# Four weight tiles parted into two words ahead of their use

## The chip, the cores and the metric

The kernel runs on one core of one Trainium2 chip. The core has five engines with queues of their own: TensorE (PE, with its weight loads PEld), VectorE (DVE), ScalarE (ACT), GpSimd (POOL) and SyncE (SP, which here only issues transfers). The metric is the device time of one launch in microseconds (us).

## What is computed

Three layers stand behind each other, on 8 batches of 576 positions and 512 features:

```
q_p, k_p = phi(q), phi(k)                 # exp(+-(x @ w_phi - max|.|)), 256 features per head
attn  = (q_p @ (k_p^T v)) / (q_p @ sum k_p + 1e-6)
gate  = sigmoid(causal depthwise convolution of attn, 5 taps)
x     = (gate * (attn @ w_val)) @ w_out
u     = x + real(fft over positions and features of x)
un    = (u - mean) / sqrt(var + 1e-6)      # over the 512 features
out   = u + relu(un @ w_ch1) @ w_ch2       # 512 -> 2048 -> 512
```

The weights `w_val`, `w_out`, `w_ch1` and `w_ch2` arrive as 64-bit floats and are made into 32-bit ones on the chip. Every product of the second and third layer works on operands parted into two words: a high word `h` in the rounded type fp32r, and a low word `l = x - h`. One product is then three matmuls, h*h, h*l and l*h (`mm3`, L77).

## The kernel before

**Stages.** The attention (`run_attention`, L1162) runs in 80 steps of a written order, and beside it all weights are converted and stored to DRAM (`conv_mlp`, L324, into `w_scr`). Then comes the mixing, a loop over batches (L1242 to L1265): for batch b+1 the convolution taps, the sigmoid and the value product (`emit_V`), for batch b the output product (`emit_W`) and the two transforms (`emit_FD`, `emit_SD`). The mixing's order on each engine is found by the tile framework, which may move an instruction past others of its engine. The last turn of that loop is `run_last` (L1001), called the tail below: transforms and output product of the last two batches, the layer norm of the first block of 512 positions (`ln_stages`) and its operands (`prep_un`). After it `run_mlp` (L1152) walks 9 blocks of 512 positions twice, once for each half of the 2048 hidden features.

**Weights of the MLP.** Each of the two MLP products multiplies 2x2 blocks with seven products in place of eight, so that a weight tile of four 128x128 quarters needs four sums of quarters beside them: `sum_w` (L329) loads the four quarters of a tile (columns 0 to 511 of a row of `w_scr`), forms the sums on POOL in place (L339 to L342), and stores all four results behind the quarters (L343). There are 32 tiles (product i, column group j of 8, half o), five after each batch of the mixing, with a buffer `ws` of two slots. Columns 128 to 1023 are the seven operands, 896 columns.

**Parting.** `prep_w` (L660) loads such a row into a buffer `wr` (two slots, a counter alternates them), rounds it to the high word on ACT (`o_hi`, L640, recorded at L66) and subtracts on DVE or POOL (`o_lo`, recorded at L72 for DVE, at L75 for POOL). In `run_last` it is called for column groups 0 and 1 of the first product, which the first MLP products need (two calls, four tiles, L1013 and L1014), and for group 2 (L1020). The rest is parted in the first block and at the change of halves.

**Order in the tail and the MLP.** `run_last` and `run_mlp` write down operations with the engines that may do them ("v" DVE, "p" POOL, "a" ACT, "d" SP's queue, "m" PE), and `place_ops` (L1071) puts them into an order by due times: of the operations that are ready on an engine, the one that is due first goes first. An operation marked "vp" is given to POOL when POOL, at twice the duration, would end it before DVE could get to it, or before it is due. The first MLP products write PSUM tiles that take the place of the tail's (`open_mlp2`), and the tail's last DVE operations read those.

**Buffers around the change.** The pool `g` holds the taps' sum `acc` (its own slots, used in the attention only; later a PSUM tile `psa` with one slot takes its place, L415), the sigmoid `sg` (two slots), its product with the values `gv` (two) and the sums and differences `gs` (two). `ident` is the identity matrix for the attention's transposes.

Of the kernel before, what the change touches and what calls it, by code (L numbers as in the profile page):

```python
# [7 lines left out]
F32 = mybir.dt.float32  # L8
F32R = mybir.dt.float32r
# [3 lines left out]
ALU = mybir.AluOpType  # L13
# [4 lines left out]
NB, NH, S, D, F = 8, 8, 576, 64, 128  # L18
DM, DFF, KC = 512, 2048, 5
NT = NB * S  # L20
HS = S // 2
# [8 lines left out]
def f32(ap):  # L30
    return ap.bitcast(F32)
# [3 lines left out]
def attention_moe_mixer_kernel(  # L35
# [18 lines left out]
    nc = tc.nc  # L54
    mm = nc.tensor.matmul

    def pool(stack, name, bufs, space=None, side=None):
        kw = {} if space is None else {"space": space}
        if side is not None:
            kw["side"] = side  # L60
        if space is not DRAM:
            kw["reuse_waits"] = "tile"
        return stack.enter_context(tc.tile_pool(name=name, bufs=bufs, **kw))

    def hi_act(dst, src):
        nc.scalar.activation(out=dst, in_=src, func=ACTF.Copy)  # L66
# [7 lines left out]
    def lo_pool(dst, src, hi):  # L74
        nc.gpsimd.tensor_tensor(out=dst, in0=src, in1=f32(hi), op=ALU.subtract)  # L75
# [8 lines left out]
    def convert(i, src, n, shape, halve, done):  # L84
        raw = P["xf"].tile([128, 1024, 2], I32, tag="xf", name="raw64")[:, 0:n]
        nc.sync.dma_start(out=raw.rearrange("p n t -> p (n t)").rearrange("p (k f) -> p k f", k=shape[0]), in_=src)
        yield
        lo32, hi32 = raw[:, :, 0].bitcast(U32), raw[:, :, 1]
        a = P["xh"].tile([128, 2, 1024], I32, tag=f"x{i % 2}", name="cv")
        ex, lo = a[:, 0, 0:n], f32(a[:, 1, 0:n])  # L90
        sg = lo
        mt = stg.tile([128, 1024], I32, tag="mt", name="mt")[:, 0:n]
        w = f32(mt)
        nc.vector.tensor_scalar(out=ex, in0=hi32, scalar1=0x7FF00000, scalar2=None, op0=ALU.bitwise_and)
        nc.scalar.activation(out=lo, in_=lo32, func=ACTF.Copy, scale=2.0 ** -32)
        yield
        nc.vector.tensor_scalar(out=mt, in0=hi32, scalar1=0xFFFFF, scalar2=0x4B000000, op0=ALU.bitwise_and, op1=ALU.bitwise_or)  # L97
        nc.scalar.activation(out=ex, in_=ex, func=ACTF.Relu, scale=8.0, bias=ebias[:, int(halve):int(halve) + 1])
        nc.gpsimd.tensor_scalar(out=w, in0=w, scalar1=-7340032.0, scalar2=None, op0=ALU.add)  # L99
        nc.gpsimd.tensor_tensor(out=w, in0=lo, in1=w, op=ALU.add)  # L100
        yield
        nc.scalar.activation(out=sg, in_=hi32, func=ACTF.Sign)
        nc.gpsimd.tensor_tensor(out=w, in0=w, in1=f32(ex), op=ALU.mult)
        nc.gpsimd.tensor_tensor(out=w, in0=w, in1=sg, op=ALU.mult)
        done(w.rearrange("p (k f) -> p k f", k=shape[0]))
        yield

    base = pool(ctx, "base", 1)
    ebias = base.tile([128, 2], F32, name="ebias")
    dram = pool(ctx, "scratch", 1, DRAM)  # L110
    ident = base.tile([128, 128], F32, name="ident")
    eps = base.tile([128, 1], F32, name="eps")
    warm = base.tile([128, 1], F32, name="warm")
    ones = base.tile([128, 128], F32R, name="ones")
    x_scr = [dram.tile([4, 128, S], F32, name=f"x_scr{b}") for b in range(NB)]
    w_scr = [dram.tile([NJ, 2, 128, 8 * 128], F32, name=f"w_scr{i}") for i in range(2)]
    un_scr = [dram.tile([128, 4, TB], F32, name=f"un_scr{t}") for t in range(NBK)]
    part_scr = [[dram.tile([128, 2, HB], F32, name=f"part_scr{t}_{q}") for q in range(4)] for t in range(NBK)]
    u_scr = [dram.tile([4, 128, S], F32, name=f"u_scr{b}") for b in range(NB)]
# [4 lines left out]
    P = {"g1": pool(ctx, "g1", 1)}  # L124
# [19 lines left out]
    vx = ExitStack()  # L144
    gx = ExitStack()
    lx = ExitStack()
    R = "right"
# [10 lines left out]
    ap1 = pool(att, "ap1", 1)  # L158
# [6 lines left out]
    ps_nm = pool(att, "ps_nm", 1, PSUM)  # L165

    wp = ap1.tile([128, F], F32, name="wp")

    raw = {}
    pj = {}  # L170
# [153 lines left out]
    def conv_mlp(n, j, i):  # L324
        def done(t):
            nc.sync.dma_start(out=w_scr[i][j][:, :, 0:512].rearrange("o p f -> p o f"), in_=t)
        return convert(n, (w_ch1, w_ch2)[i][j].bitcast(I32).rearrange("o p f -> p o f"), 1024, (2,), False, done)

    def sum_w(n):  # L329
        for k in ((0, 1) if n == 0 else (n + 1,)):  # L330
            if k < len(wsteps):
                i, j, o = wsteps[k]
                wsum[k] = t = P["ws"].tile([128, 512], F32, tag="ws", name="ws")
                nc.sync.dma_start(out=t, in_=w_scr[i][j, o][:, 0:512])
        i, j, o = wsteps[n]
        t = wsum.pop(n)
        a21, a11, a12, a22 = (t[:, k * 128:(k + 1) * 128] for k in range(4))
        tt = nc.gpsimd.tensor_tensor
        tc.keep_in_program_order(tt(out=a22, in0=a21, in1=a22, op=ALU.add))  # L339
        tt(out=a21, in0=a11, in1=a21, op=ALU.subtract)  # L340
        tt(out=a11, in0=a22, in1=a11, op=ALU.subtract)
        tt(out=a12, in0=a12, in1=a11, op=ALU.subtract)  # L342
        nc.sync.dma_start(out=w_scr[i][j, o][:, 512:1024], in_=t)  # L343

    def conv_taps(i):
        def done(t):
# [23 lines left out]
    def open_mix():  # L370
        P["g0"] = pool(gx, "g0", 1, side=R)
        P["ws"] = pool(vx, "ws", 2, side=R)
        P["psv"] = pool(vx, "psv", 2, PSUM, side=R)
        P["psa"] = pool(vx, "psa", 1, PSUM, side=R)

# [11 lines left out]

    wsteps = [(i, j, o) for j in range(NJ) for i in range(2) for o in range(2)]
    wsum = {}
    xf = {}  # L390
    xhl = {}
    geo = {}
# [20 lines left out]
    def tap_steps(b, m):  # L413
        x = xf[b]
        if "psa" in P:  # L415
            acc = P["psa"].tile([128, 2, 512], F32, tag="pa", name="acc")[:, :, 0:HS]
        else:
            acc = P["g"].tile([128, 2, HS], F32, tag="acc", name="acc")

        def shifted(t):  # L420
            return x[:, m, t:t + S].rearrange("p (a s) -> p a s", a=2)
        nc.scalar.activation(out=acc, in_=shifted(4), func=ACTF.Copy, scale=cw[:, m, 4:5])  # L422
        for t in range(4):
            nc.vector.scalar_tensor_tensor(  # L424
                out=acc, in0=shifted(t), scalar=cw[:, m, t:t + 1], in1=acc, op0=ALU.mult, op1=ALU.add
            )
            if t < 3:
                yield
        taps[b, m] = acc
        yield  # L430

    def emit_taps(b, m):
        drain(tap_steps(b, m))

    def emit_V(b, m):
        h, l = xhl[b]
        if m == 0:
            geo[b] = tuple(P[f"g{b % 2}"].tile([128, 4, 2, NE], F32R, tag=f"g{i}", name="ge") for i in range(2))
        if (b, m) not in taps:
            emit_taps(b, m)  # L440
        t = taps.pop((b, m))
        acc = P["g"].tile([128, S], F32, tag="sg", name="sg")
        nc.scalar.activation(out=acc.rearrange("p (a s) -> p a s", a=2), in_=t, func=ACTF.Sigmoid)
        gv = P["g"].tile([128, S + 2], F32, tag="gv", name="gv")
        for n in range(2):
            p = P["psv"].tile([128, HS], F32, tag="ps", name="val")
            sl = slice(n * HS, (n + 1) * HS)
            for c in range(4):
                ws = slice(m * 128, (m + 1) * 128)
                mm3(p, (wv[0][:, c, ws], wv[1][:, c, ws]), (h[:, c, sl], l[:, c, sl]), c == 0, c == 3)  # L450
            nc.vector.tensor_tensor(out=gv[:, sl], in0=p, in1=acc[:, sl], op=ALU.mult)
        nc.vector.tensor_copy(out=gv[:, S:S + 1], in_=gv[:, 0:1])
        gs = P["g"].tile([128, 2, NE], F32, tag="gs", name="gs")
        for a, op in ((0, ALU.add), (1, ALU.subtract)):
            nc.vector.tensor_tensor(out=gs[:, a, :], in0=gv[:, 0:NE], in1=gv[:, S:S - NE:-1], op=op)  # L455
        gh, gl = geo[b]
        hi_act(gh[:, m], gs)
        lo_pool(gl[:, m], gs, gh[:, m])
        if m == 3:
            xhl.pop(b)  # L460
            xf.pop(b)
# [115 lines left out]
    NJP = NJ // 2  # L577
    NH_SLOTS = 7
    blocks = [(0, t) for t in range(NBK)] + [(1, t) for t in reversed(range(NBK))]
    wt = [[], []]  # L580
# [71 lines left out]
    def o_dma(pairs, r, w, kb, e="d"):  # L652
        def f(e):
            for o, x in pairs:
                (nc.sync if e == "d" else nc.scalar).dma_start(out=o, in_=x)
        op(e, 0, f, r, w, max(0.5 * len(pairs), K["bw"] * kb) if e == "d" else 0.5 * len(pairs), K["dl"] + 0.0028 * kb)
# [2 lines left out]

    def prep_w(i, j, e):  # L660
        for o in range(2):
            b = wcount[0] % 2
            wcount[0] += 1
            h, l = wt[i][j % NJP][o]
            raw = wr[b]
            r = raw.rearrange("p q f -> p (q f)")
            wk = [("w", i, j % NJP, o, k) for k in range(2)]
            o_dma([(r, w_scr[i][j, o, :, 128:1024])], [], [("wr", b)], 448)
            o_hi(h, raw, 896, [("wr", b)], [wk[0]])
            o_lo(e, l, raw, h, 896, [("wr", b), wk[0]], [wk[1]])  # L670
            yield
# [699 lines left out]
```

## Time and profile before

| | |
|---|---|
| runs timed | 1438.33, 1440.83, 1443.11 us, median 1440.83 |
| the profiled execution | 1442.91 us |
| its span, first to last instruction | 1441.1 us |
| granted TensorE clock, mean | 0.979 of full speed |
| PE / PEld busy | 1352.5 us (94%) / 1301.8 us (90%) |
| DVE busy | 1247.2 us (87%) |
| ACT busy | 814.1 us (56%) |
| POOL busy | 707.0 us (49%) |
| transfers | 187 MB, 130 GB/s in the mean |

How to read it: the busy shares are means over stages that have different limits. The attention ends near 340 us, the mixing runs to about 607 us, the tail from there to about 657 us, and the MLP from there to the end. All times in rows are microseconds from the start of the span, unless they are marked ns.

### The profile page before, as it was taken

The page shows a single profiled execution, that of the slowest core. Times are in us where ns is not written, and L with a number is a line of the kernel's source. Part 1 is how long each engine was busy: PE and PEld are TensorE (multiplying, and loading weights), DVE is VectorE, ACT ScalarE, POOL GpSimd, SP SyncE. Part 2 cuts the span into 40 slices and gives each one's busy share as a digit, 9 for nine tenths or more (in the row PEclk, how much of TensorE's full clock was granted, in tenths as well). Part 3 has the DMA queues.
Part 4 walks back from the last instruction along what each step waited for, and adds up shares of the span by engine and source line. Part 5 has one row for each costly group of instructions (what it writes and reads, how often), then busy time and mean ns, then how long its engine had stood idle before and what let it go on. Part 6 is the DMA issues. An engine that isn't in the chain of part 4 may idle for free.

```text
span 1441.1 us, 35040 instructions
## 1 busy us (share of the span) xinstructions
PE 1352.5 (94%) x14672; PEld 1301.8 (90%) x14672; DVE 1247.2 (87%) x1938; ACT 814.1 (56%) x1513; POOL 707.0 (49%) x526
## 2 busy tenths in 40 slices
PE   6899999997999999986899899999999999999998
PEld 5788888887999999986899899999999999999998
DVE  6689999886999989798999999999899887788776
ACT  4778888764545545464555555555555555444442
POOL 3858888721667666563655655545436111111111
PEclk9999999998999999988899999999999999999999
DMA  6457777741333432236322332232343222222211
GB/s 231 148 187 252 270 273 267 244 173 35 132 133 140 144 135 100 91 112 214 132 89 89 118 104 87 75 116 89 116 125 101 81 81 66 83 88 89 88 38 51
DMA packets 89851, 186.98 MB, mean 130 GB/s; under 512 B 10455, under 2 KB 37335, under 8 KB 87518
## 3 DMA queue, kind: packets, MB, share of 16 engines
q1 hardware_dynamic: 88488, 181.33, 37.0%
q10 hardware_dynamic: 1206, 3.41, 0.6%
q8 instruction: 115, 1.88, 0.5%
q14 instruction: 42, 0.34, 0.1%
HBM read 121.79 MB, written 62.93 MB: 128 GB/s over the span
## 4 chain that ended last, share of the span: by engine, by line
PE 44%; DVE 32%; issue 7%; POOL 7%; ACT 5%; DMA 4%; SPq 0%; DVEq 0%; POOLq 0%; ACTq 0%
PE cx L875 9%; PE x L806 9%; PE cy L875 5%; PE y L806 4%; DVE acc L424 4%; DVE A L647 3%; DVE c L647 3%; PE kv L243 3%; PE z L806 3%; PE nm L282 2%; DVE acc L647 2%; PE pj L204 2%; PE cz L875 2%; DVE s L751 2%; DVE gs L455 2%
## 5 line engine op out<-in xcount | busy, mean ns | idle before, releaser
L875 PE MATMUL cx<-h,w 128*128 128x256 f32 x1152 | 176.2, 286 | 4.8 <-ACT h L66 2.5
L875 PEld LDWEIGHTS cx<-h,w 128*128 128x128 f32 x1152 | 158.2, 194 | 6.7 <-ACT h L66 3.1
L66 ACT ACTIVATE h<-c 128x512 fp32r<-128x512 f32 x180 | 111.6, 627 | 39.7 <-DVE c L647 22.4
L647 POOL TENSOR_TENSOR c<-c,c 128x512 f32<-128x512 f32 x35 | 49.8, 1422 | 165.2 <-ACT h L650 125.6
L647 DVE TENSOR_TENSOR acc<-cx,acc 128x512 f32<-128x512 f32 x144 | 98.0, 681 | 33.7 <-PE cx L875 33.0
L650 ACT ACTIVATE c<-c 128x512 f32<-128x512 f32 x108 | 67.9, 630 | 99.9 <-DVE c L647 98.5
L806 PE MATMUL x<-un,w 128*128 128x256 f32 x864 | 117.2, 285 | 6.5 <-DVE eo L647 5.8
L75 POOL TENSOR_TENSOR h<-c,h 128x512 fp32r<-128x512 f32 x33 | 48.3, 1466 | 149.2 <-ACT h L66 149.0
L875 PE MATMUL cy<-h,w 128*128 128x256 f32 x864 | 117.3, 284 | 3.1 <-DVE h L72 1.9
L806 PEld LDWEIGHTS x<-un,w 128*128 128x128 f32 x864 | 109.9, 193 | 7.2 <-issue 6.0
L424 DVE SCALAR_TENSOR_TENSOR acc<-xf,cw,acc 128x576 f32<-128x576 f32 x128 | 105.0, 820 | 11.9 <-ACT acc L422 10.8
L875 PEld LDWEIGHTS cy<-h,w 128*128 128x128 f32 x864 | 108.9, 191 | 5.6 <-DVE h L72 2.5
L243 PE MATMUL kv<-vraw,ke 128*64 128x66 f32 x2560 | 97.2, 229 | 13.8 <-ACT ke L222 11.1
L243 PEld LDWEIGHTS kv<-vraw,ke 128*64 128x64 f32 x2560 | 84.4, 140 | 25.7 <-ACT ke L222 12.0
L72 DVE TENSOR_TENSOR h<-c,h 128x512 fp32r<-128x512 f32 x111 | 103.9, 937 | 1.3 <-ACT h L66 0.7
L211 DVE TENSOR_REDUCE m<-pj 128x8 f32<-128x1024 f32 (+1 forms) x80 | 88.7, 1108 | 10.3 <-PE pj L204 10.3
L204 PE MATMUL pj<-wp,kqraw 64*128 64x128 f32 x1152 | 88.8, 292 | 5.4 <-DMA kqraw<-in_k_dram 4.4
L204 PEld LDWEIGHTS pj<-wp,kqraw 64*128 64x128 f32 x1152 | 73.0, 192 | 19.2 <-issue 18.1
L214 DVE TENSOR_TENSOR y<-pj,m 128x1024 f32<-128x1024 f32 (+1 forms) x80 | 88.7, 1108 | 0.4
L282 PE MATMUL nm<-kvT,qe 128*64 128x65 f32 x2304 | 84.6, 226 | 3.1 <-DVE xs L293 1.6
L75 POOL TENSOR_TENSOR ge<-gs,ge 128x580 fp32r<-128x580 f32 x32 | 46.8, 1462 | 78.7 <-ACT ge L66 78.7
L99 POOL TENSOR_SCALAR mt<-mt 128x1024 f32<-128x1024 f32 (+1 forms) x21 | 55.7, 2651 | 59.9 <-DVE mt L97 42.5
(249 smaller groups left out, 4244.0 us busy)
## 6 DMA issues: line engine op xcount, KB each, us to landing
raw<-in_w_ch_dram SPq DMA_DIRECT2D x16, 1024.0 KB, 7.1
wr<-w_scr SPq DMA_DIRECT2D x32, 448.0 KB, 3.5
vraw<-in_v_dram SPq DMA_DIRECT2D x16, 660.0 KB, 8.6
x_scr<-xT SPq DMA_DIRECT2D x32, 288.0 KB, 5.9
xf<-x_scr SPq DMA_DIRECT2D x8, 1152.0 KB, 5.9
out_dram<-acc SPq DMA_DIRECT2D x36, 256.0 KB, 2.2
kqraw<-in_k_dram SPq DMA_DIRECT2D x15, 576.0 KB, 7.7
kqraw<-in_q_dram SPq DMA_DIRECT2D x15, 576.0 KB, 6.2
```

Of the source, the lines that this page charges most:

```text
L66: nc.scalar.activation(out=dst, in_=src, func=ACTF.Copy)
L72: nc.vector.tensor_tensor(out=dst, in0=src, in1=f32(hi), op=ALU.subtract)
L75: nc.gpsimd.tensor_tensor(out=dst, in0=src, in1=f32(hi), op=ALU.subtract)
L204: mm(p[:, h, o:o + F], t[r, w, 128 * c:128 * c + 128], wp[r, :], start=True, stop=True)
L211: nc.vector.tensor_reduce(out=m, in_=pv, axis=AX.X, op=ALU.max, apply_absolute_value=True)
L214: nc.vector.tensor_tensor(out=y, in0=pv, in1=m.unsqueeze(3).to_broadcast([128, 2, 2 * n, F]), op=ALU.subtract)
L243: mm(t[p, w, :], e[:, a, h, j, p], tv[:, h, slot, :], start=slot % 5 == 0 and w == 0, stop=slot % 5 == 4 and w == 3, skip_group_check=True)
L282: mm(t[p, 2 * j + h, 0:65], e[:, a, h, j, p], kt[:, 2 * h + a, b, :], start=(a == 0), stop=(a == 1))
L424: nc.vector.scalar_tensor_tensor(out=acc, in0=shifted(t), scalar=cw[:, m, t:t + 1], in1=acc, op0=ALU.mult, op1=ALU.add)
L647: op(e, cols, lambda e: (nc.vector if e == "v" else nc.gpsimd).tensor_tensor(out=o, in0=x, in1=y, op=alu), r, w)
L806: mm(p[:, n], l, v[:, kt], start=first and n + kt + m == 0, stop=kt == 1 and m == 2, skip_group_check=True)
L875: mm(p[:, o], v, r[:, n], start=first and o + n + m == 0, stop=n + m == 3, skip_group_check=True)
```

## The change

The four tiles of the first product's column groups 0 and 1 (the test is `parted`, L331 of the changed kernel) are parted during the mixing. `sum_w` puts its four sums behind the quarters in a buffer `ws` that is twice as wide (1024 columns, still two slots) and stores only the sums. For the four tiles it stores nothing; it rounds columns 128 to 1023 into a new buffer `wh` (one slot) on ACT. The next call of `sum_w` begins with `part_w`: POOL subtracts in place, and SP stores both words to a new DRAM scratch `w_hl`. Only then the next tile's load is issued. `prep_w` has for these tiles two plain loads of the words straight into their places, without ACT, DVE, POOL or `wr`.

To make room, three tiles give way: `ident` lies in a pool that ends with the attention, the taps' `acc` of the attention takes slots of `gv`, and the sigmoid `sg` has one slot in place of two.

```diff
--- before.py
+++ after.py
@@ -108,12 +108,12 @@
     base = pool(ctx, "base", 1)
     ebias = base.tile([128, 2], F32, name="ebias")
     dram = pool(ctx, "scratch", 1, DRAM)
-    ident = base.tile([128, 128], F32, name="ident")
     eps = base.tile([128, 1], F32, name="eps")
     warm = base.tile([128, 1], F32, name="warm")
     ones = base.tile([128, 128], F32R, name="ones")
     x_scr = [dram.tile([4, 128, S], F32, name=f"x_scr{b}") for b in range(NB)]
     w_scr = [dram.tile([NJ, 2, 128, 8 * 128], F32, name=f"w_scr{i}") for i in range(2)]
+    w_hl = [dram.tile([2, 2, 2, 128, 7 * 128], F32, name="w_hl0")]
     un_scr = [dram.tile([128, 4, TB], F32, name=f"un_scr{t}") for t in range(NBK)]
     part_scr = [[dram.tile([128, 2, HB], F32, name=f"part_scr{t}_{q}") for q in range(4)] for t in range(NBK)]
     u_scr = [dram.tile([4, 128, S], F32, name=f"u_scr{b}") for b in range(NB)]
@@ -165,6 +165,7 @@
     ps_nm = pool(att, "ps_nm", 1, PSUM)
 
     wp = ap1.tile([128, F], F32, name="wp")
+    ident = ap1.tile([128, 128], F32, name="ident")
 
     raw = {}
     pj = {}
@@ -326,21 +327,44 @@
             nc.sync.dma_start(out=w_scr[i][j][:, :, 0:512].rearrange("o p f -> p o f"), in_=t)
         return convert(n, (w_ch1, w_ch2)[i][j].bitcast(I32).rearrange("o p f -> p o f"), 1024, (2,), False, done)
 
+
+    def parted(i, j):
+        return i == 0 and j < 2
+
+    def load_ws(n):
+        if n < len(wsteps):
+            i, j, o = wsteps[n]
+            wsum[n] = t = P["ws"].tile([128, 1024], F32, tag="ws", name="ws")
+            nc.sync.dma_start(out=t[:, 0:512], in_=w_scr[i][j, o][:, 0:512])
+
+    def part_w():
+        if parting:
+            i, j, o, r, h = parting.pop()
+            l = r.bitcast(F32R)
+            lo_pool(l, r, h)
+            nc.sync.dma_start(out=w_hl[i][j, o, 0], in_=f32(h))
+            nc.sync.dma_start(out=w_hl[i][j, o, 1], in_=f32(l))
+
     def sum_w(n):
-        for k in ((0, 1) if n == 0 else (n + 1,)):
-            if k < len(wsteps):
-                i, j, o = wsteps[k]
-                wsum[k] = t = P["ws"].tile([128, 512], F32, tag="ws", name="ws")
-                nc.sync.dma_start(out=t, in_=w_scr[i][j, o][:, 0:512])
+        if n == 0:
+            load_ws(0)
         i, j, o = wsteps[n]
         t = wsum.pop(n)
-        a21, a11, a12, a22 = (t[:, k * 128:(k + 1) * 128] for k in range(4))
+        part_w()
+        load_ws(n + 1)
+        a21, a11, a12, a22, b21, b11, b12, b22 = (t[:, k * 128:(k + 1) * 128] for k in range(8))
         tt = nc.gpsimd.tensor_tensor
-        tc.keep_in_program_order(tt(out=a22, in0=a21, in1=a22, op=ALU.add))
-        tt(out=a21, in0=a11, in1=a21, op=ALU.subtract)
-        tt(out=a11, in0=a22, in1=a11, op=ALU.subtract)
-        tt(out=a12, in0=a12, in1=a11, op=ALU.subtract)
-        nc.sync.dma_start(out=w_scr[i][j, o][:, 512:1024], in_=t)
+        tc.keep_in_program_order(tt(out=b22, in0=a21, in1=a22, op=ALU.add))
+        tt(out=b21, in0=a11, in1=a21, op=ALU.subtract)
+        tt(out=b11, in0=b22, in1=a11, op=ALU.subtract)
+        tt(out=b12, in0=a12, in1=b11, op=ALU.subtract)
+        if not parted(i, j):
+            nc.sync.dma_start(out=w_scr[i][j, o][:, 512:1024], in_=t[:, 512:1024])
+            return
+        h = P["wh"].tile([128, 896], F32R, tag="wh", name="wh")
+        r = t[:, 128:1024]
+        hi_act(h, r)
+        parting.append((i, j, o, r, h))
 
     def conv_taps(i):
         def done(t):
@@ -370,6 +394,7 @@
     def open_mix():
         P["g0"] = pool(gx, "g0", 1, side=R)
         P["ws"] = pool(vx, "ws", 2, side=R)
+        P["wh"] = pool(vx, "wh", 1, side=R)
         P["psv"] = pool(vx, "psv", 2, PSUM, side=R)
         P["psa"] = pool(vx, "psa", 1, PSUM, side=R)
 
@@ -387,6 +412,7 @@
 
     wsteps = [(i, j, o) for j in range(NJ) for i in range(2) for o in range(2)]
     wsum = {}
+    parting = []
     xf = {}
     xhl = {}
     geo = {}
@@ -415,7 +441,7 @@
         if "psa" in P:
             acc = P["psa"].tile([128, 2, 512], F32, tag="pa", name="acc")[:, :, 0:HS]
         else:
-            acc = P["g"].tile([128, 2, HS], F32, tag="acc", name="acc")
+            acc = P["g"].tile([128, S + 2], F32, tag="gv", name="acc")[:, 0:S].rearrange("p (a s) -> p a s", a=2)
 
         def shifted(t):
             return x[:, m, t:t + S].rearrange("p (a s) -> p a s", a=2)
@@ -439,7 +465,7 @@
         if (b, m) not in taps:
             emit_taps(b, m)
         t = taps.pop((b, m))
-        acc = P["g"].tile([128, S], F32, tag="sg", name="sg")
+        acc = P["g"].tile([128, S], F32, tag="sg", name="sg", bufs=1)
         nc.scalar.activation(out=acc.rearrange("p (a s) -> p a s", a=2), in_=t, func=ACTF.Sigmoid)
         gv = P["g"].tile([128, S + 2], F32, tag="gv", name="gv")
         for n in range(2):
@@ -659,12 +685,18 @@
 
     def prep_w(i, j, e):
         for o in range(2):
+            wk = [("w", i, j % NJP, o, k) for k in range(2)]
+            if parted(i, j):
+                for k in range(2):
+                    t = wt[i][j][o][k].rearrange("p q f -> p (q f)")
+                    o_dma([(f32(t), w_hl[i][j, o, k])], [], [wk[k]], 448)
+                yield
+                continue
             b = wcount[0] % 2
             wcount[0] += 1
             h, l = wt[i][j % NJP][o]
             raw = wr[b]
             r = raw.rearrange("p q f -> p (q f)")
-            wk = [("w", i, j % NJP, o, k) for k in range(2)]
             o_dma([(r, w_scr[i][j, o, :, 128:1024])], [], [("wr", b)], 448)
             o_hi(h, raw, 896, [("wr", b)], [wk[0]])
             o_lo(e, l, raw, h, 896, [("wr", b), wk[0]], [wk[1]])
```

## Rows read from the trace of the kernel before

**Rows 1.** Windows: length, then busy us (count) of PE, PEld, DVE, ACT, POOL; clock, DMA

```profile
372.00:600.00 228.00, 222.30 (x1653) 217.91 (x1653) 209.94 (x374) 116.37 (x253) 157.65 (x189) 0.99 0.37 128
...
614.40:656.90 42.50, 31.57 (x198) 29.61 (x197) 40.89 (x61) 23.91 (x49) 24.73 (x14) 0.84 0.37 133
656.90:685.00 28.10, 21.62 (x148) 20.93 (x149) 23.39 (x32) 15.56 (x25) 9.70 (x7) 0.86 0.60 192
```

**Rows 2.** The chain that ended last, a piece of the tail (start, length, what)

```profile
617.79 1.91 DVE w L72
```

**Rows 3.** Timeline of PE, first MLP product (start, us, operation, [idle before, releaser])

```profile
656.90 2.90 PE L806 MATMUL x<-un,w 128*128 128x256 f32 x12 [5.76 <-DVE eo L647]
```

**Rows 4.** Timeline of DVE in the tail and behind it

```profile
614.45 0.76 DVE L647 TENSOR_TENSOR s<-A 128x256 f32<-128x256 f32 x2 [0.65 <-DMA A<-u_scr]
...
617.79 1.91 DVE L72 TENSOR_TENSOR w<-wr,w 128x896 fp32r<-128x896 f32 x1 [1.24 <-ACT w L66]
619.62 0.41 DVE L72 TENSOR_TENSOR sl<-s,sh 128x256 fp32r<-128x256 f32 x1
...
625.75 1.16 DVE L72 TENSOR_TENSOR sl<-s,sh 128x256 fp32r<-128x256 f32 x1
...
627.20 1.63 DVE L72 TENSOR_TENSOR w<-wr,w 128x896 fp32r<-128x896 f32 x1
...
647.10 4.42 DVE L72 TENSOR_TENSOR un<-T,un 128x512 fp32r<-128x512 f32 x2
...
652.04 0.68 DVE L72 TENSOR_TENSOR un<-A,un 128x512 fp32r<-128x512 f32 x1
...
669.81 1.09 DVE L72 TENSOR_TENSOR w<-wr,w 128x896 fp32r<-128x896 f32 x1 [1.30 <-ACT w L66]
```

**Rows 5.** Timeline of POOL in the tail

```profile
616.62 2.13 POOL L75 TENSOR_TENSOR w<-wr,w 128x896 fp32r<-128x896 f32 x1 [4.64 <-ACT w L66]
...
624.46 2.16 POOL L75 TENSOR_TENSOR w<-wr,w 128x896 fp32r<-128x896 f32 x1 [1.43 <-ACT w L66]
626.88 0.99 POOL L647 TENSOR_TENSOR s<-T 128x256 f32<-128x256 f32 x1 [0.26 <-ACT T L650]
...
646.59 1.86 POOL L647 TENSOR_TENSOR u<-eo 128x574 f32<-128x574 f32 x1
648.41 2.56 POOL L75 TENSOR_TENSOR wg<-wr,wg 128x896 fp32r<-128x896 f32 x1
```

**Rows 6.** Timeline of ACT in the tail

```profile
616.80 0.95 ACT L66 ACTIVATE w<-wr 128x896 fp32r<-128x896 f32 x1
...
617.95 0.41 ACT L66 ACTIVATE sh<-s 128x256 fp32r<-128x256 f32 x1
```

**Rows 7.** Timeline of SP in the tail (the second row's length holds its waits)

```profile
609.42 0.37 SPq L655 DMA_DIRECT2D A<-u_scr  x1
609.84 41.47 SPq L655 DMA_DIRECT2D wr<-w_scr  x8
```

**Rows 8.** Mixing: sums by line (busy us, mean ns | idle before), min/median/max ns by line

```profile
L455 DVE TENSOR_TENSOR gs<-gv 128x290 f32<-128x290 f32 x51 | 39.1, 806 | 0.5
...
L455 DVE TENSOR_TENSOR gs<-gv x56: 446/458/1704, 370.9 to 608.9; 128x290 f32<-128x290 f32 x56
...
L550 DVE TENSOR_TENSOR u<-eo 128x578 f32<-128x578 f32 x12 | 13.4, 1124 | 0.0
...
L550 DVE TENSOR_TENSOR u<-eo x12: 748/1146/1900, 408.9 to 591.5; 128x578 f32<-128x578 f32 x12
```

**Rows 9.** Waits in the mixing (waiter <- releaser: us in total, times, longest)

```profile
PE val L80 <- POOL xh L75: 5.0, 9, 1.4
```

**Rows 10.** Timelines of ACT and DVE, one sigmoid ahead of the products before it

```profile
502.47 0.65 ACT L443 ACTIVATE sg<-acc 128x576 f32<-128x576 f32 x1 [0.41 <-DVE acc L424]
...
503.24 0.73 ACT L422 ACTIVATE acc<-xf,cw 128x576 f32<-128x576 f32 x1
...
510.42 0.82 DVE L451 TENSOR_TENSOR gv<-val,sg 128x288 f32<-128x288 f32 x2
```

## The prediction

> **What bounds the kernel now.** I read the windows first, then the chain of waits, then the timelines of single engines in the tail, and last the sums by line in the mixing. In the windows the reader sees two stages that the change touches [rows 1]. In the mixing (372 to 600 us) PE is busy 222.3 of 228 us and DVE 209.9: both are near full, POOL is busy 157.7, ACT 116.4. In the tail (614.4 to 656.9 us, from the layer norm's first addition to the first MLP product) the picture turns: DVE is busy 40.9 of 42.5 us, PE only 31.6, and the granted clock falls to 0.84. So the tail is DVE's. The chain of waits says the same: from 617.79 on it runs over DVE, beginning with the low word of a weight tile [rows 2]. The first MLP product starts at 656.90, after PE stood idle 5.76 us for the tail's last DVE operation, `eo` [rows 3]. Whatever leaves DVE between 614.45 and 656.9 lets the MLP start earlier. Behind that, DVE is busy 23.4 of 28.1 us [rows 1] with the next weights and the next layer norm; it keeps its backlog, so an earlier start moves all of it.
>
> **What the change takes from the tail.** Four high words on ACT and four low words, two on DVE and two on POOL, go. ACT is busy 23.9 of 42.5 us; its 4 x 0.95 us are worth nothing by themselves, but one of them stood between the layer norm's sum and its rounding `sh` at 617.95 [rows 6], which feeds the first `sl`.
> - On DVE the two low words took 1.91 and 1.63 us [rows 4], 3.54 us together. The undisturbed price is 1.09 us (669.81, same rows). The rest was time beside POOL: the first ran while POOL's own low word held from 616.62 to 618.75, the second while POOL's addition held from 626.88 to 627.87 [rows 5].
> - On POOL the two low words took 2.13 and 2.16 us [rows 5]. The second ended at 626.62, and the `sl` on DVE that began at 625.75 took 1.16 us where its like took 0.41 (619.62) [rows 4]: 0.75 us of DVE go with it.
>
> Sum for DVE: 3.54 + 0.75 = 4.3 us, less about 0.3 for an addition that may meet POOL elsewhere: 4.0 us, bounded by 2 x 1.09 = 2.2 below.
> - The two low words of group 2 (`wg`) are moved as well. Their buffers `wr` are no longer taken by the four tiles, so their loads can follow the words at once, and their low words can run on POOL near 625 us. The second one ran at 648.41 for 2.56 us beside two `un` low words that took 4.42 us where one alone takes 0.68 [rows 4, 5]; POOL's `u` before it held until 648.45, so about 4.42 - 1.36 - 1.35 = 1.7 us of it is the weight's. The planner may put another POOL operation there; I take 1.0 us, bounds 0 and 1.7.
>
> Tail: -5.0 us, from -2.2 to -6.0.
>
> **SP's queue in the tail.** The load of `A` is issued at 609.42, then weight loads that wait for `wr`, eight in 41.47 us [rows 7]. After the change eight loads of 448 KB wait for nothing and follow `A` directly, 3.67 MB in place of 1.8. None is needed before the first product, some 40 us later, so their own time is hidden. The price would be a later `A`: it landed 5.0 us after its issue, just before 614.45, when DVE had waited 0.65 us for it [rows 4]. I take 0; bounds 0 and 3 (a rival below).
>
> **What it adds to the mixing.** The four adds on POOL stay, out of place instead of in place, at the same size: nothing. Two tiles are parted beside each of the first two batches.
> - ACT: 4 x 0.95 = 3.8 us on an engine that is busy half the time [rows 1, 6]: nothing, unless it waits for the sums.
> - POOL: 4 x 2.15 = 8.6 us [rows 5], beside 158 busy us of 228. POOL alone has room. Behind it wait PE's value products, which stood 5.0 us in all for POOL's `xh` [rows 9], and DVE, which stands when an operation with two SBUF inputs meets POOL. How often, the sums say: `gs` took 39.1 us for 51 where 51 x 0.458 = 23.4 is undisturbed, `u` 13.4 us for 12 where 12 x 0.748 = 9.0 is [rows 8], so 15.7 + 4.4 = 20.1 us for 157.7 us of POOL, 0.13 us for each. 8.6 us more of POOL cost DVE 1.1 us, and with DVE at 92% and PE at 97% nearly all of that shows: +1.0 us, bounds 0 and 8.6 (every low word in DVE's way for its full length).
>
> The Trainium skill, page "SBUF — State Buffer", section "Who interferes with whom", says that a DVE instruction with two SBUF inputs and a GpSimd one that reads SBUF exclude each other, and that the one that comes second blocks until the first is done. The trace agrees: the 4.42 us pair above ends only when POOL's two instructions have. By that rule alone, with no share of chance, the added low words would cost 8.6 us and the change would lose.
> - The sigmoid's single slot: before, `sg` of the next chunk often ran ahead of the product that read the last one. At 502.47 a sigmoid ran 8.8 us before the two products at 510.42 that still read its predecessor ended [rows 10]; comparing all 31 successive pairs of these two lines, 17 ran ahead, by 0.3 to 10.5 us. With one slot each waits. It is needed only for the next product, so it is not late itself; but the tap sum `psa` is free for the following chunk only after it, and the taps are what DVE fills gaps with. The price per pair lies between 0 and the ACT steps that now stand between product and taps, 0.65 + 0.73 = 1.4 us [rows 10], so 0 to 24 us; DVE has other work nearly always, so I take the end near 0: +1.0 us.
> - SP: the next `ws` load stands behind two stores that wait for POOL's low word, and two transfers of 448 KB replace one of 256 KB at four tiles. The load was needed several us later; +0.3 us, bounds 0 and 4.
> - `ident` and `acc` move without adding a wait: `acc` is read by the sigmoid before `gv` needs its slot.
>
> Mixing: +2.3 us.
>
> **Sum.** -5.0 + 2.3 = -2.7 us. Against the profiled execution, 1442.91 us (its span 1441.1 and 1.8 around it), that is 1440.2; that execution lies 2.1 us above the median of the runs, 1440.83, so I forecast 1438.1 us. The likeliest case's own range runs from -6.0 with the mixing's terms at nothing (1434.8) to -3.0 with 4.0 in the mixing (1441.8). About 0.3% (4.3 us) is what a measurement of this kernel can tell from no change: faster means below 1436.5, slower above 1445.2.
>
> **Rivals.**
> 1. The mixing hides its additions (PE's steady pace sets it, the sigmoids lose nothing), and the tail gains more, because a shorter tail keeps PE's clock up (0.84 now) and the `wg` words leave DVE's way: -6 - 1.5 = -7.5, 1433.3 us. For it: PE at 97% in the mixing; against: DVE at 92% there. Chance 0.23.
> 2. The lock in the mixing in full: +8.6, +1.3 for the other terms, -5.0: +4.9, 1445.7 us. It decides from a mixing loss of 9.3 us. Against it the rate of 0.13. This is the page's rule without chance. Chance 0.06.
> 3. The sigmoid's slot: 17 pairs at half of 1.4 us are 11.9; with 1.3 for the rest and -5.0 it is +8.2, 1449 us. It is slower than the bound from 8 us on, when two thirds of a us are lost at 12 of the pairs. For it: the taps are the largest DVE line of the mixing. Chance 0.10.
> 4. The weight words delay `A` by 3 us or the layer norm's chain of waits, not DVE's sum, paces the tail: the gain shrinks to 1.5, +2.3: 1441.6 us. Against it: DVE was never idle after 617.79. The Trainium skill, page "DMA: Bandwidth & Descriptors", section "Queues, rings and completion order", has descriptors consumed in ring order; by that `A` goes first. Chance 0.13.
>
> **Chances.** Forecast 0.48, rivals 0.23, 0.06, 0.10, 0.13. Faster: rival 1 and a fifth of the forecast's case, 0.32. Slower: rivals 2 (part of it) and 3, 0.14. Within 0.3%: 0.54. The range takes in rival 1 with its own scatter and stops short of rival 3: 1432 to 1445.
>
> **What would show it.** In the changed trace: no low word of group 0 or 1 on DVE or POOL after 607 us; the stretch from the first `s` addition to the first MLP product about 37.5 us in place of 42.5, its DVE still full; `A` landing at 5 us. In the mixing four 896-column operations on POOL and ACT near 375 to 425 us, `gs` mean hardly above 806 ns, and the stretch from the first sigmoid to the last val product 1 to 3 us longer. The prediction is wrong if the mixing grows by over 5 us, or if the tail shrinks by less than 2.

## The result and the profile after

The changed kernel takes 1450.45 us in the median (1450.11 to 1452.15, 4 runs) against 1441.09 (1438.33 to 1443.11). The ratio is 1.0066, 95% interval 1.0047 to 1.0085: slower by some 9 us, past the bound of 0.3% and outside the range that was forecast (1432 to 1445).

Three marks cut both profiles into stages: the first sigmoid on ACT, the issue of `A`'s load on SP, and the first MLP product on PE. These are the rows of the timelines of ACT, SP and PE after.

```profile
334.52 0.69 ACT L469 ACTIVATE sg<-acc 128x576 f32<-128x576 f32 x1
...
619.19 0.37 SPq L681 DMA_DIRECT2D A<-u_scr  x1
619.60 4.88 SPq L681 DMA_DIRECT2D w<-w_hl  x8
...
664.16 2.93 PE L838 MATMUL x<-un,w 128*128 128x256 f32 x12 [8.26 <-DVE r L673]
```

Before, the marks stood at 335.37, 609.42 [rows 7] and 656.90 [rows 3]. All profiles of this study, in us:

| kernel | to the first sigmoid | mixing (to `A`'s load) | tail (to the first product) | rest | span |
|---|---|---|---|---|---|
| before | 335.4 | 274.1 | 47.5 | 784.2 | 1441.1 |
| after | 334.5 | 284.7 | 45.0 | 784.4 | 1448.6 |
| e1, after, second sum held | 334.5 | 272.2 | 45.6 | 782.9 | 1435.2 |
| e2, before, one sigmoid slot | 337.0 | 272.6 | 47.8 | 783.3 | 1440.7 |
| e3, after without parting | 333.4 | 284.0 | 46.8 | 784.6 | 1448.8 |
| e4, e3 with second sum held | 337.4 | 272.2 | 46.8 | 783.9 | 1440.3 |
| e5, e3 with three ws slots | 338.1 | 280.0 | 46.7 | 783.5 | 1448.2 |
| e6, before, no hold | 339.3 | 281.6 | 46.8 | 784.1 | 1451.8 |
| e7, e1 with two sigmoid slots | 338.5 | 274.8 | 46.5 | 784.1 | 1443.8 |
| e8, e1 with `wo` words on POOL | 337.8 | 272.2 | 47.4 | 785.4 | 1442.7 |

Each row is one execution. The first column varies by 6 us, and by 3.3 us already between e1 and e8, whose code is the same up to the tail; a difference of 2 or 3 us between whole spans is therefore not read as an effect here, and the stages are compared one by one. Before to after the tail gave 2.5 us and the mixing took 10.6.

Where the mixing lost them is seen first in the windows of after: in the same 228 us, PE did 1578 matmuls where it had done 1653 [rows 1].

```profile
372.00:600.00 228.00, 214.46 (x1578) 209.18 (x1577) 198.37 (x350) 113.70 (x245) 158.39 (x184) 0.99 0.38 133
...
624.24:664.16 39.92, 28.31 (x198) 26.73 (x196) 35.79 (x58) 21.58 (x46) 20.16 (x13) 0.92 0.50 186
```

DVE and PE are both less busy, so neither is the new bound. The waits of the mixing name POOL: PE stood 10.1 us for its `xh` words, 5.0 before [rows 9]. That is 5.1 of the 10.6 us. PE's idle time in the whole stage rose by 7.8 us (it was busy 262.4 of 274.1 us before and 265.2 of 284.7 after), so this wait is the largest part of the loss, not all of it.

```profile
ACT sg L469 <- DVE gv L477: 17.9, 6, 4.5
...
POOL ws L357 <- DMA ws<-w_scr: 10.9, 3, 4.8
POOL ws L358 <- DMA ws<-w_scr: 10.2, 7, 2.8
PE val L80 <- POOL xh L75: 10.1, 10, 2.5
```

L357 to L360 are the four sums, of which the first two (L357, L358) wait for loads. They stood 21 us for their loads; in the kernel before, only the first sum did, for 2.4 us (its sums by line in the mixing, busy, mean ns, idle before):

```profile
L339 POOL TENSOR_TENSOR ws<-ws 128x128 f32<-128x128 f32 x32 | 18.4, 576 | 2.4 <-DMA ws<-w_scr 2.4
L340 POOL TENSOR_TENSOR ws<-ws 128x128 f32<-128x128 f32 x32 | 16.2, 506 | 2.0
```

The chain of waits of after shows the place: loads and stores of `ws` lie on it, 13 of them among its pieces over 1.2 us, where the chain of before has one store and one load. Three of those pieces are shown first, then the timeline of POOL, which shows how they come about.

```profile
426.00 5.76 DMA ws<-w_scr
...
456.75 2.65 DMA ws<-w_scr
...
464.03 5.15 DMA ws<-w_scr
```

```profile
494.54 0.47 POOL L357 TENSOR_TENSOR ws<-ws 128x128 f32<-128x128 f32 x1
495.09 0.46 POOL L359 TENSOR_TENSOR ws<-ws 128x128 f32<-128x128 f32 x1
497.95 0.69 POOL L358 TENSOR_TENSOR ws<-ws 128x128 f32<-128x128 f32 x1 [2.40 <-DMA ws<-w_scr]
498.61 0.67 POOL L360 TENSOR_TENSOR ws<-ws 128x128 f32<-128x128 f32 x1
499.77 1.45 POOL L75 TENSOR_TENSOR ge<-gs,ge 128x580 fp32r<-128x580 f32 x1 [0.48 <-ACT ge L66]
```

Between L357 and L360 of one tile stands L358, the second sum, of the next tile, and waits for a load that has just been issued. L360 of the older tile, which has its data, stands behind it; so do the store of that tile and the load into its slot. Here PE loses nothing at once, as `ge` still waits for ACT. Where POOL owes PE a word, PE does lose. The next rows show such a place, on POOL, ACT and PE: ACT had been making the high words of `xh` since 504.62, but the second sum stood 2.77 us for its load, five more sums stood behind it, and POOL's first low word of `xh` began only at 507.97. PE stood 1.51 us for it.

```profile
504.40 0.94 POOL L358 TENSOR_TENSOR ws<-ws 128x128 f32<-128x128 f32 x1 [2.77 <-DMA ws<-w_scr]
505.31 0.46 POOL L359 TENSOR_TENSOR ws<-ws 128x128 f32<-128x128 f32 x1
...
507.97 4.16 POOL L75 TENSOR_TENSOR xh<-xf,xh 128x576 fp32r<-128x576 f32 x3
...
504.62 2.42 ACT L66 ACTIVATE xh<-xf 128x576 fp32r<-128x576 f32 x4 [1.35 <-PE val L81]
...
509.42 0.40 PE L80 MATMUL val<-xh,wv 128*128 128x288 f32 x1 [1.51 <-POOL xh L75]
```

**Why the order changed.** Before, the second sum wrote over `a21`, which the first reads; that made it wait for the first, and the first is held at its written place by `keep_in_program_order`. So the hold carried over to all four. After, the sums lie out of place, the second writes `b21` and needs nothing but the load. The framework was free to move it, and moved it ahead; by what estimate, the rows don't show. In the rows of tile `ws` (count, min/median/max ns, first and last start) the first start tells it: before, the second sum (L340) began at 374.5 us, just behind the first (L339); after, the second (L358) begins at 327.1 us, 45 us ahead of the first (L357). First the rows of before, then those of after.

```profile
L339 POOL TENSOR_TENSOR ws<-ws x32: 455/466/997, 373.9 to 598.2; 128x128 f32<-128x128 f32 x32
L340 POOL TENSOR_TENSOR ws<-ws x32: 454/462/982, 374.5 to 598.8; 128x128 f32<-128x128 f32 x32
```

```profile
L358 POOL TENSOR_TENSOR ws<-ws x32: 454/463/945, 327.1 to 599.5; 128x128 f32<-128x128 f32 x32
L357 POOL TENSOR_TENSOR ws<-ws x32: 449/463/983, 372.3 to 608.6; 128x128 f32<-128x128 f32 x32
```

### The profile page after: what moved, and what is told of

Its sections match the earlier page's. It is cut to its first block, busy times and chain, and to the rows that moved or that the text cites. A ratio compares the mean times of both kernels' runs of the same rounds, so it can differ in the third digit from the quotient of the medians.

```text
span 1448.6 us, 35055 instructions
## 1 busy us (share of the span) xinstructions
PE 1352.8 (93%) x14672; PEld 1301.4 (90%) x14672; DVE 1240.0 (86%) x1935; ACT 815.3 (56%) x1513; POOL 710.6 (49%) x529
## 4 chain that ended last, share of the span: by engine, by line
PE 47%; DVE 28%; POOL 7%; DMA 7%; issue 6%; ACT 5%; SPq 0%; DVEq 0%; POOLq 0%; ACTq 0%
PE cx L907 9%; PE x L838 8%; PE cy L907 5%; PE y L838 4%; DVE A L673 3%; DVE c L673 3%; PE kv L244 3%; PE z L838 2%; PE nm L283 2%; DVE acc L450 2%; DVE acc L673 2%; PE cz L907 2%; DVE s L783 2%; PE pj L205 2%; DMA ws<-w_scr 2%
## 5 line engine op out<-in xcount | busy, mean ns | idle before, releaser
L450 DVE SCALAR_TENSOR_TENSOR acc<-xf,cw,acc 128x576 f32<-128x576 f32 x128 | 105.0, 820 | 12.2 <-ACT acc L448 10.9
L244 PE MATMUL kv<-vraw,ke 128*64 128x66 f32 x2560 | 96.4, 228 | 11.7 <-ACT ke L223 10.6
L205 PEld LDWEIGHTS pj<-wp,kqraw 64*128 64x128 f32 x1152 | 73.4, 193 | 19.7 <-issue 17.8
L80 PE MATMUL val<-xh,wv 128*128 128x288 f32 x256 | 78.3, 307 | 10.1 <-POOL xh L75 10.1
```

The lines of the kernel that those rows point to most:

```text
L80: mm(o, ah, bl, start=False, stop=False)
L205: mm(p[:, h, o:o + F], t[r, w, 128 * c:128 * c + 128], wp[r, :], start=True, stop=True)
L244: mm(t[p, w, :], e[:, a, h, j, p], tv[:, h, slot, :], start=slot % 5 == 0 and w == 0, stop=slot % 5 == 4 and w == 3, skip_group_check=True)
L450: nc.vector.scalar_tensor_tensor(out=acc, in0=shifted(t), scalar=cw[:, m, t:t + 1], in1=acc, op0=ALU.mult, op1=ALU.add)
```

## The experiments

Theory 1: the floating second sum. Theory 2: the sigmoid's single slot (rival 3 of the prediction, which had priced it at 1449 us). Theory 3: the parting's own work in the mixing. Each kernel was timed in five rounds beside the kernel before (1441.57 us for e1 to e4, 1439.25 for e5 to e8).

**e1, the second sum held.**

```diff
-        tt(out=b21, in0=a11, in1=a21, op=ALU.subtract)
+        tc.keep_in_program_order(tt(out=b21, in0=a11, in1=a21, op=ALU.subtract))
```

> The changed kernel with one more sum held at its place in POOL's order: the second one, b21 = a11 - a21, is kept behind the first as the first is kept behind what stands ahead of it. Theory 1 (with the sums out of place the second no longer depends on the first, floats ahead in POOL's order, and stands there for its load, 21 us of POOL waits for ws loads in place of 2.4): the mixing loses most of its 10.6 us of growth, some 1442 us, and POOL's waits for ws loads fall to about 3 us. Theory 2 (the sigmoid's single slot) and theory 3 (the parting's own work on ACT, POOL and the queue): no change, 1450 us.

Measured: 1438.59 us, ratio 0.9992 (0.9972 to 1.0012). One line takes back all 10.6 us of the mixing, and 2 us more (272.2). The sums by line on POOL in the mixing of e1:

```profile
L359 POOL TENSOR_TENSOR ws<-ws 128x128 f32<-128x128 f32 x32 | 16.2, 505 | 0.0
L358 POOL TENSOR_TENSOR ws<-ws 128x128 f32<-128x128 f32 x32 | 15.9, 498 | 0.0
L357 POOL TENSOR_TENSOR ws<-ws 128x128 f32<-128x128 f32 x32 | 15.8, 495 | 7.3 <-DMA ws<-w_scr 7.3
...
L75 POOL TENSOR_TENSOR ws<-ws,wh 128x896 fp32r<-128x896 f32 x4 | 9.0, 2254 | 3.6 <-ACT wh L66 3.6
```

The second sum waits for nothing, and PE's wait for `xh` falls to 3.5 us. The first sum still stands 7.3 us for loads, more than the expected 3 and than the 2.6 of e4, which parts no tile; PE's wait is short all the same.

**e2, the kernel before with one sigmoid slot.**

```diff
-        acc = P["g"].tile([128, S], F32, tag="sg", name="sg")
+        acc = P["g"].tile([128, S], F32, tag="sg", name="sg", bufs=1)
```

> The kernel before with one slot for the sigmoid in place of two, and nothing else. Theory 2: it costs 6 to 10 us, 1447 to 1451 us, all of it in the mixing. Theories 1 and 3: within 2 us of the kernel before, 1441 us.

Measured: 1443.46 us, ratio 1.0021 (1.0003 to 1.0039). ACT's waits for `gv` rise to 17.8 us as in the changed kernel, but the mixing is 272.6 us, no longer than before. Theory 2 falls as the cause; what the interval leaves for the slot is 0.4 to 5.6 us.

**e3 and e4, no parting; without and with the second sum held.** Both change `parted`; e4 has e1's line as well.

```diff
-        return i == 0 and j < 2
+        return False
```

> The changed kernel with no tile parted ahead: wide ws, sums out of place, the sigmoid's one slot, the moved tiles, but the tail loads and parts its four tiles as before. Theory 1: the mixing still grows by 6 to 10 us and the tail is back at 42.5 us, 1448 to 1452 us. Theory 2: the same. Theory 3: as the kernel before, 1441 us.

> The same without parting, and the second sum held behind the first. Theory 1: as the kernel before, 1441 us within 2. Theory 2: 1447 to 1451 us. Theory 3: 1441 us. Theory 1 is told from 3 by the run without parting and without the hold, and from 2 by this one.

Measured: e3 1453.76 us, ratio 1.0096 (1.0071 to 1.0121); e4 1443.62, 1.0018 (1.0003 to 1.0033). With no tile parted the loss is there in full, and the hold takes it away: 284.0 to 272.2 us in the mixing. Rows of POOL and of the waits in the mixing, e3 first:

```profile
L358 POOL TENSOR_TENSOR ws<-ws 128x128 f32<-128x128 f32 x30 | 15.1, 503 | 16.7 <-DMA ws<-w_scr 15.2 <-issue 1.5
...
PE val L80 <- POOL xh L75: 11.5, 8, 2.9
```

```profile
L358 POOL TENSOR_TENSOR ws<-ws 128x128 f32<-128x128 f32 x32 | 16.1, 502 | 0.0
...
PE val L80 <- POOL xh L75: 2.4, 6, 0.6
```

For `xh` PE waited 11.5 us in e3 and 2.4 in e4, its weight loads beside it 13.6 and 4.2. The mixing's 272.2 us are the same with parting (e1) and without (e4): theory 3 falls, the parting's own work there costs nothing that this can tell. e4 also keeps the wide `ws`, the sums out of place, the sigmoid's one slot and the moved tiles, so none of these makes the mixing longer either.

**e5, three slots for `ws`, each load a tile earlier** (e3's kernel).

```diff
-        P["ws"] = pool(vx, "ws", 2, side=R)
+        P["ws"] = pool(vx, "ws", 3, side=R)
...
-        load_ws(n + 1)
+        load_ws(n + 2)
```

> The kernel without parting, the second sum free to float, but ws with three slots and each load issued one tile earlier (u256 lies in another buffer to make room). It was 1453.8 us with two slots, its mixing 284 us from the first sigmoid to the load of A. If the wait of the floating sum for its load is the price (theory 1a), POOL's waits for ws loads go under 5 us and the mixing is back at 272 to 276 us, some 1442 to 1445 us. If the order itself is the price (1b: sums standing ahead of ge and xh words though their data is there), the mixing stays at 280 us or more, 1449 us and up.

Measured: 1451.49 us, ratio 1.0088 (1.0056 to 1.0121), mixing 280.0. Its 280.0 us lie at the mark that was set for 1b, but it doesn't tell 1a from 1b: the wait, 21.5 us in e3, was to go away and grew to 22.7, all of it at the second sum. In the rows of `ws` that sum first starts at 330.4 us, 46 us ahead of the first sum (376.7), so it floated on to the earlier load.

```profile
POOL ws L359 <- DMA ws<-w_scr: 22.7, 11, 3.8
```

(L359 is the second sum in this kernel.) A third slot was no cure for a sum that can still move ahead of its load.

**e6, the kernel before without its hold.**

```diff
-        tc.keep_in_program_order(tt(out=a22, in0=a21, in1=a22, op=ALU.add))
+        tt(out=a22, in0=a21, in1=a22, op=ALU.add)
```

> The kernel before with the hold on its first sum taken away, sums in place as they were. Theory 1: all four sums float ahead and stand for their loads; the mixing grows by 8 to 12 us, 1449 to 1453 us. If the change's out-of-place sums or wide buffers cost time in another way, this stays at 1441 us.

Measured: 1453.92 us, ratio 1.0102 (1.0080 to 1.0123). With the old in-place sums and narrow buffers the same loss appears once nothing holds them; the mixing grows by 7.5 us, just under the 8 to 12 that were expected. The first sum's waits in e6:

```profile
L339 POOL TENSOR_TENSOR ws<-ws 128x128 f32<-128x128 f32 x30 | 16.2, 541 | 37.6 <-DMA ws<-w_scr 37.4
```

**e7, e1 with the sigmoid's second slot** (`u256` lies in the buffer `fs` to make room).

```diff
-        acc = P["g"].tile([128, S], F32, tag="sg", name="sg", bufs=1)
+        acc = P["g"].tile([128, S], F32, tag="sg", name="sg")
```

> The changed kernel with the second sum held, and the sigmoid's second slot given back (u256 lies in another buffer to make room). What is left of theory 2 (the before kernel with one slot was 0.2% slower) gives 2 to 3 us: 1436 us against the 1438.6 of the held kernel. If the slot is worth nothing, 1438 to 1439 us, and ACT's waits for gv go away without the mixing getting shorter than 272 us.

Measured: 1442.70 us, ratio 1.0019 (1.0003 to 1.0036), not faster than e1. ACT's waits for `gv` fall from 10.7 us in e1 to 5.3, and the mixing is no shorter (274.8). The slot is worth nothing that can be measured. One more thing shows here: the first sum stands 10.2 us for its loads in e7, nearly the 10.9 of the changed kernel, yet its mixing is 9.9 us shorter. So a first sum that stands that long does not by itself bring the loss.

**e8, e1 with the low words of group 3 on POOL alone.**

```diff
-                wg = chain(*(prep_w(*w, K["w"]) for w in ws))
+                wg = chain(*(prep_w(*w, "p" if w == (0, 3) else K["w"]) for w in ws))
```

> The changed kernel with the second sum held, and the two low words of column group 3 given to POOL alone. In the changed kernel both stand on DVE ahead of the first MLP product (2.08 us), in the kernel before only one did. If that is where part of the tail's gain went, A's load to first product falls by about 1 us, to 44.0 to 44.6 from 45.6, and the kernel to 1437.5 us. If the layer norm's chain paces the tail, it stays at 45 to 46 us, and the block after it loses what POOL's slower words cost: 1438.6 to 1440 us.

Measured: 1444.47 us, ratio 1.0038 (1.0021 to 1.0055), tail 47.4. Taking two operations from DVE made the tail longer by 1.8 us, not shorter by one. Neither expected case came: the second had 45 to 46 us and at most 1440. The traces show where the time went. POOL held the two `wo` words for 4.99 us, and the two DVE operations beside them took 2.55 and 2.56 us, where e1 has 0.68 each. First POOL and DVE in e8, then DVE in e1:

```profile
648.02 4.99 POOL L75 TENSOR_TENSOR wo<-wr,wo 128x896 fp32r<-128x896 f32 x2
648.53 2.55 DVE L673 TENSOR_TENSOR T<-A,T 128x512 f32<-128x512 f32 x1
651.00 2.56 DVE L72 TENSOR_TENSOR un<-T,un 128x512 fp32r<-128x512 f32 x1
```

```profile
645.28 0.68 DVE L673 TENSOR_TENSOR T<-A,T 128x512 f32<-128x512 f32 x1
645.89 0.68 DVE L72 TENSOR_TENSOR un<-T,un 128x512 fp32r<-128x512 f32 x1
...
647.15 2.08 DVE L72 TENSOR_TENSOR wo<-wr,wo 128x896 fp32r<-128x896 f32 x2
```

DVE saved 2.08 us and lost 3.75; the difference makes up 1.7 of the 1.8 us. Its waits for PE's means and ACT's root are 2.3 us in both kernels, so they are not the difference.

## Why the prediction was wrong

**The step that failed** is a sentence of the mixing: "The four adds on POOL stay, out of place instead of in place, at the same size: nothing." The size is right (462 ns before and 463 after, in the median); the place is not. The overwritten operand was what tied the second sum to the held first one. The mixing took 10.6 us more, and that is shown from both sides to come from the order: holding the second sum takes away some 12 us of mixing with parting (after to e1) and without (e3 to e4), and taking the hold from the kernel before adds 7.5 (e6). In the four profiles in which a sum can float (after, e3, e5, e6) the mixing took 280.0 to 284.7 us, in the other six 272.2 to 274.8. That POOL's wait for the loads is how it costs is read from the rows, where PE's wait for `xh` is 10.1 to 12.2 us in those four and 2.4 to 6.8 in the other six; e5, which was to take the wait alone away, did not, so that link was not tested by itself.

**Rival 3 came near the time by another way.** 1449 us was priced for the sigmoid's slot. Its sign in the trace is there (17.9 us of ACT waiting for `gv`), but e2 has the same wait with no longer mixing, and e7 has less of it with no shorter one. A rival whose number fits is not shown by that.

**The mixing's other terms held.** The parting there was put at 1.0 us for DVE; e1 and e4 differ by nothing that single executions can tell. The four low words took 2.16 us each, as priced. `gs` has a mean of 809 ns after, 806 before [rows 8].

**The tail gave 2.5 us, not 5.0.** DVE's work shrank by 5.1 us, from 40.89 busy us [rows 1] to 35.79, close to the sum. The parts differ, so that is partly luck: the four tiles' low words gave 3.5 as priced, the `sl` and `un` words some 4.4 where 1.75 was priced (one of each moved to POOL), and the products `A<-A,s` and a second `wo` word ahead of the first MLP product took 2.3 back. But DVE's idle time rose from 1.6 to 4.1 us, 2.3 of it in the layer norm's chain (for PE's means and ACT's root) and 1.4 for ACT's copies of the output product. The timeline of DVE after:

```profile
630.64 1.28 DVE L673 TENSOR_TENSOR A<-A,mean 128x512 f32<-128x512 f32 x2 [0.94 <-PE mean L754]
...
639.06 0.95 DVE L783 RECIPROCAL s<-s 128x128 f32<-128x128 f32 x1 [1.05 <-ACT s L676]
...
654.28 1.90 DVE L72 TENSOR_TENSOR un<-T,un 128x512 fp32r<-128x512 f32 x1
656.11 1.75 DVE L72 TENSOR_TENSOR un<-A,un 128x512 fp32r<-128x512 f32 x1
```

The reading is that the low words had filled these waits, and with them gone the waits are bare. The other traces bear it out: the 2.3 us for means and root stand in all three parted kernels looked at (after, e1, e8) and in none without parting (before, e3, e4). That is half of rival 4, which was given 0.13. The `wg` words did run earlier (637.31 and 641.54 on POOL), but two `un` words still meet POOL operations: 1.90 and 1.75 us where one alone takes 0.68 [rows 4]. Against the same kernel without parting the gain is smaller still, 1.8 us (e3 to after) and 1.2 (e4 to e1), as e3 and e4 have 46.8 us where the kernel before has 47.5. Rival 1 expected a shorter tail to keep the granted clock up. It was 0.84 before and 0.92 after, but 0.89 in e4, which has the longer tail, so that link is not shown. `A` landed 5.05 us after its issue, as forecast, with eight loads behind it.

**The rest** moved with its start: 784.2 and 784.4 us, as assumed.

With the order mended (e1) the change does what the working said in sign: the tail is 1.9 us shorter than before and the mixing no longer, and the kernel is level with the one before within 0.3%. Against the same kernel without parting (e4, 1443.62) its 1438.59 us are 5 us less, but in the profiles 2.9 us of that lie before the mixing, where both are alike. It beats the changed kernel; that any variant beats the kernel before is not shown.

## What to carry to other kernels

Where a scheduler orders instructions by what depends on what, an edit from in place to out of place removes a dependence, and with it an order that a hold on one instruction had given to all behind it. Before calling such an edit free, look up which instruction each one was waiting for, and look in the trace after for the same line's first start: a line that begins 45 us earlier than it did has come loose. And work taken from a full engine is gained only as far as its chain has no waits that the work had covered.

## What the hardware showed that was not expected

A `ws` load of 256 KB took 2.9 us in the median of the changed kernel (2.6 to 5.8, where the profile shows the landing). On its chain of waits seven such loads lie. Four took 2.5 to 2.9 us. The other three were each issued just behind a load of 1152 KB (`xf`) on the same queue: 0.46 us behind it, at 426.00, 5.76 us; 1.8 us behind it, at 464.03, 5.15 us; 1.9 us behind it, at 541.09, 4.58 us. From the timeline of SP, then from the chain:

```profile
425.54 0.37 SPq L426 DMA_DIRECT2D xf<-x_scr  x1
...
462.22 0.37 SPq L426 DMA_DIRECT2D xf<-x_scr  x1
...
539.18 0.38 SPq L426 DMA_DIRECT2D xf<-x_scr  x1
```

```profile
541.09 4.58 DMA ws<-w_scr
```

All three waits of the first sum in the mixing, 4.83, 4.14 and 1.89 us, are for these three loads. So the price of a sum that stands for its load depended here on what the queue carried just ahead.
